# A convolution and feed-forward kernel on one core: the first windows of x, the dummies and the copies of the prologue in another order

## The chip, the cores and the metric

The kernel runs on one core of a Trainium2 chip. Its metric is the device time of one execution in microseconds (us). A core has five engines with a queue each: TensorE (PE in the profile; PEld is its loading of stationary operands), VectorE (DVE), ScalarE (ACT), GpSimd (POOL) and SyncE (SP). They run side by side and wait for each other by semaphores. Besides, 16 DMA engines move data. The letter q behind an engine's name stands for its instruction sequencer.

## The reference

```python
def _attn_ref(x, weight):                  # x: (8, 3904, 192), weight: (8 heads, 7 taps)
    w = softmax(weight, over the taps)
    x_pad = zeros(6 rows) + x              # along the sequence
    out[b, s, h, g] = sum_k w[h, k] * x_pad[b, s + k, h, g]        # 24 channels per head

def _moe_ref(x, w1, w2, w3, w_out):        # x: (31232, 192), d_ff = 1024
    a = x @ w1
    b = x @ w2
    h = a * b @ w3
    return h @ w_out
```

A causal depthwise convolution of 7 taps goes first, then a product of two projections, then two matrices that can be multiplied with each other ahead of time. All inputs and the output are float32; the kernel computes in bfloat16 and accumulates in float32.

## The kernel before

The 31232 tokens are cut into two streams of 15616 (`NS = 2`, index r). In most tiles the two streams sit side by side, one on each half of the partitions. The work runs in rounds R of 512 tokens per stream.

**Convolution.** x comes in windows of 32 rows that overlap by 6, so that each gives 26 new tokens. A banded 32x32 matrix per head, `Aband`, is the stationary operand (`conv`, L275); it is built in the prologue from the softmax of the taps: `share`, `spread` (PE, L215), `wsb`, `cprod`, `bps` (PE, L236), and the copy to `Aband` by VectorE at L240. The result in PSUM (`cps`) is copied to `convo` (L283). Windows go in batches; batch 0 has 20 windows per stream, all in one tile `xb`.

**The first windows of batch 0.** Windows below `HW = 8` come as float32 over SP's queue into the tile `begin`: window 0 apart (L149, 26 rows, since 6 rows are zeros set by VectorE at L141) and windows 1 to 7 in one transfer (L144), each for both streams. Three casts at L232 take them into `xb`: ScalarE casts stream 0 whole and the second half of stream 1, VectorE the first half of stream 1. Windows 8 to 19 come over POOL's queue straight into `xb` (L117, cast on the way), and behind them the weights `wn` (L187 to L190). In VectorE's queue the cast of L232 stands right ahead of the copy to `Aband`.

**Transposes.** The convolution's result is turned for the first product. For batch 0, `first_transposes` (L332) has a PSUM tile `tps` for each of three groups of channels k; for batches 1 and 2, `pe_transposes` (L317) puts the 15 transposes of all three groups in one tile `tps`, and three copies (L330) take them to `xT[0]` (VectorE), `xT[1]` (ScalarE) and `xT[2]` (VectorE), in this order. Later batches go through DRAM and DMA transposes.

**First product** (`first_product`, L378): for each of 8 blocks of 128 hidden channels, `pa` and `pb` (6 matmuls each, two streams side by side on half of the rows), `pa` copied to `asb` by ScalarE (L385), `abT = asb * pb` by VectorE (L387). Since the streams sit on different halves of the partitions, each weight tile `wn[k]` has an exchanged twin `ws` (`swap_w`, L181: two copies of 64x256 per stretch of columns). **Second product** (`second_product`, L403): `abT` times the folded `W_sb`. The fold of w3 and w_out (`w3_transpose` L448/L451, `w3_product` L460) is spread over rounds 1 and 2.

**PSUM.** All PSUM tiles are taken in turn from four buffers (`banks`); a PE group waits until the copy that reads the tile four places earlier is done.

**Order.** It is written out by hand (`tc.manual_schedule()`): each engine's queue holds its instructions in the order of the code. `first_product(R, between)` calls the entries of `between` behind the given block. `warm(n, wd)` (L192, matmuls at L195) issues n dummy matmuls on zeros.

Of the kernel before, what the change touches and what calls it, by code (L numbers as in the profile page):

```python
# [16 lines left out]
def kernel(  # L17
# [10 lines left out]
    nc = tc.nc  # L28
# [8 lines left out]
    NS = 2  # L37
# [6 lines left out]
    NP = D // Q  # L44
    C = 32
    ST = C - PAD
# [6 lines left out]
    NB = len(SIZES)  # L53
    FIRST = [sum(SIZES[:b]) for b in range(NB)]
    MAXN = 20
    HW = 8

    def tok(i):
        return (i // WB) * S + (i % WB) * ST
# [8 lines left out]
    def banks(name):  # L68
        return psum.tile([128, NS, CH], FP32, tag="banks", name=name)

    def banks_bf16(name):
        return psum.tile([128, 16, 128], BF16, tag="banks", name=name)
# [8 lines left out]
    def shape_of(b):  # L81
        n = SIZES[b] // 4
        m = n // (1 if b < 3 else 2)
        return n, m, n // m
# [6 lines left out]
    def group(r, e):  # L91
        return slice((2 * r + e) * C, (2 * r + e) * C + C)

    def runs_of(b, js, e):
        n, m, E = shape_of(b)
        runs = []
        for s, i in enumerate(FIRST[b] + j * n + u * E + e for j in js for u in range(m)):
            if i < HW or i == NWIN - 1:
                continue
# [37 lines left out]
    nc.scalar.dma_start(out=taps, in_=weight)  # L137
    begin = work.tile([128, HW, D], FP32, tag="abT", bufs=LAG + 1, name="begin")
    zeros = const.tile([128, CH], BF16)
    nc.vector.memset(zeros, 0.0)  # L140
    nc.vector.memset(begin[:, 0, :], 0.0)  # L141
    for r in range(NS):
        p = group(r, 0).start
        nc.sync.dma_start(out=begin[p:p + C, 1:HW, :], in_=bass.AP(  # L144
            tensor=x.tensor, offset=(r * TS + ST - PAD) * D,
            ap=[[D, C], [ST * D, HW - 1], [1, D]]))
    for r in range(NS):
        p = group(r, 0).start
        nc.sync.dma_start(out=begin[p + PAD:p + C, 0, :], in_=x_rows[r * TS:r * TS + ST, :])  # L149

    diag = const.tile([128, 128 + 8], BF16)
# [2 lines left out]
        out=diag, in_=diag, pattern=[[-1, 128 + 8]], compare_op=ALU.is_equal,  # L154
# [13 lines left out]
    for i in range(4):  # L168
        d = diag[i * C:i * C + C, i * C + 2 * i:i * C + 2 * i + C]
        nc.vector.tensor_copy(  # L170
            out=cmask[i * C:i * C + C],
            in_=bass.AP(tensor=d.tensor, offset=d.offset, ap=[d.ap[0], [1, 2], [1, C]]))
# [6 lines left out]
    def swap_w(k, lo, hi, f, halves=(1, 0)):  # L179
        for h in halves:  # L180
            f(out=wsw[k][Q * h:Q * h + Q, lo:hi], in_=wn[k][Q - Q * h:2 * Q - Q * h, lo:hi])  # L181

    V, A, P = nc.vector.tensor_copy, nc.scalar.copy, nc.gpsimd.tensor_copy
# [8 lines left out]
    def warm(n, wd=CH):  # L192
        t = banks("warm")
        for j in range(n):
            nc.tensor.matmul(t[:, j % 2, 0:wd], zeros[:, 0:128], zeros[:, 0:wd],  # L195
                             start=True, stop=True)

    warm(6)

    low = const.tile([H, 1], FP32)  # L200
    total = const.tile([H, 1], FP32)
# [3 lines left out]
    for i in range(4):  # L205
        ps = slice(i * C, i * C + C)
        nc.vector.tensor_copy(out=every[ps],
                              in_=diag[ps, ps].unsqueeze(1).to_broadcast([C, 4, C]))
    nc.vector.reciprocal(out=total, in_=total)
    nc.vector.scalar_tensor_tensor(  # L210
        out=share[:, :, 0:K], in0=taps.unsqueeze(1).to_broadcast([H, H, K]), scalar=total,
        in1=diag[0:H, 0:H].unsqueeze(2).to_broadcast([H, H, K]), op0=ALU.mult, op1=ALU.mult)
    spread = banks("spread")
    for i in range(4):
# [5 lines left out]
        out=wsb, in_=spread[:, 0, 0:2 * H].rearrange("p (h k) -> p h k", h=H)  # L220
# [5 lines left out]
        out=cprod.rearrange("p h k (s two) -> p h k s two", two=2),  # L226
# [3 lines left out]
        op=ALU.mult)  # L230
    for r, w0, w1, f in ((0, 0, HW, A), (1, HW // 2, HW, A), (1, 0, HW // 2, V)):
        f(out=xb_of[0][0][0][group(r, 0), w0:w1, :], in_=begin[group(r, 0), w0:w1, :])  # L232
    Aband = const.tile([128, H, C], BF16)
    bps = banks("bps")
    for k in range(2):
# [3 lines left out]
            start=(k == 0), stop=(k == 1))  # L239
    nc.vector.tensor_copy(out=Aband,  # L240
                          in_=bps[:, 0, 0:C * H].rearrange("p (h s) -> p h s", s=C))
    warm(3, 256)
    swap_w(0, 0, 256, V)


    xT = [const.tile([128, RING], BF16, name=f"xT{k}", tag=f"xT{k}") for k in range(NP)]
# [4 lines left out]
    def segments(c0, n):  # L251
        out = []
        while n:
            m = min(n, Q - c0 % Q)
            out.append((c0 // Q, c0 % Q, m))
            c0, n = c0 + m, n - m
        return out

    def conv(b, h0, nh, evict=(nc.scalar.copy,), es=None):
        n, m, E = shape_of(b)  # L260
        es = range(E) if es is None else es
        if b not in convo_of:
            convo_of[b] = work.tile([128, n, NP, NS, Q], BF16, tag="convo", bufs=2, name="convo")
            heads_left[b] = H * E
        convo = convo_of[b]
        wd = nh * G
        cps = {e: banks("cps") for e in es}
        for q in range(nh):
            cs = slice((h0 + q) * G, (h0 + q + 1) * G)
            for j in range(4):  # L270
                xb, s = xb_of[b][j]
                for e in es:
                    for r in range(NS):
                        o = cps[e][j * C:j * C + C, r, 0:m * wd]
                        nc.tensor.matmul(  # L275
                            o.rearrange("p (w g) -> p w g", g=wd)[:, :, q * G:(q + 1) * G],
                            Aband[group(r, e), h0 + q, :], xb[group(r, e), s:s + m, cs],
                            start=True, stop=True)
        for f, e in zip(evict, es):
            src = cps[e][:, :, 0:m * wd].rearrange("p r (w g) -> p r w g", g=wd)  # L280
            o = 0
            for k, c0, c in segments(h0 * G, wd):
                f(out=convo[:, e::E, k, :, c0:c0 + c]  # L283
                    .rearrange("p w r g -> p r w g"), in_=src[:, :, :, o:o + c])
                o += c
        heads_left[b] -= nh * len(es)
        if not heads_left[b]:
            del xb_of[b]
# [28 lines left out]
    def pe_transposes(b):  # L317
        n = SIZES[b] // 4
        convo = convo_of[b]
        tps = banks_bf16("tps")  # L320
        for k in range(NP):
            for w in range(n):
                nc.tensor.transpose(
                    out=tps[:, k * n + w, :],
                    in_=convo[:, w, k].rearrange("p r g -> p (r g)"), identity=ident)
        t0 = tok(FIRST[b])
        for k in range(NP):
            dst = xT[k][:, t0:t0 + 4 * n * ST].rearrange("p (c w s) -> p c w s", c=4, w=n)
            src = tps[:, k * n:(k + 1) * n, :].rearrange("p w (c s) -> p c w s", c=4)
            (nc.scalar.copy if k == 1 else nc.vector.tensor_copy)(out=dst, in_=src[:, :, :, 0:ST])  # L330

    def first_transposes():  # L332
        n = SIZES[0] // 4
        convo = convo_of[0]
        for k, f in enumerate((nc.scalar.copy, nc.vector.tensor_copy, nc.vector.tensor_copy)):
            tps = banks_bf16("tps")
            for w in range(n):
                nc.tensor.transpose(  # L338
                    out=tps[:, w, :],
                    in_=convo[:, w, k].rearrange("p r g -> p (r g)"), identity=ident)  # L340
            f(out=xT[k][:, 0:4 * n * ST].rearrange("p (c w s) -> p c w s", c=4, w=n),
              in_=tps[:, 0:n, :].rearrange("p w (c s) -> p c w s", c=4)[:, :, :, 0:ST])
# [125 lines left out]

    conv(0, 0, 4, evict=(A,))
    conv(0, 4, 4, evict=(V,))  # L470
    warm(2)
    first_transposes()
    for k, h in ((2, 1), (1, 1), (2, 0)):
        swap_w(k, 0, 256, A, (h,))
    swap_w(1, 0, 256, V, (0,))
    for k in (0, 2):
        swap_w(k, 256, HC, V)
    load_x(1)
# [20 lines left out]
    def later_loads():  # L499
# [10 lines left out]
        4: seq((conv, 1, 0, 4)),  # L510
        5: seq((conv, 1, 4, 4)),
        6: seq((pe_transposes, 1)),
        7: seq((conv, 2, 0, 4))})
    first_product(1, {
        0: seq((conv, 2, 4, 4)),
        2: seq((pe_transposes, 2), (store, 2, LAG_ROWS // ST)),
        3: seq((fold, 0)),
        6: seq((fold, 2)),
# [81 lines left out]
```

## Time and profile before

| what | us |
|---|---|
| median of 3 runs | 527.73 (527.26 to 529.17) |
| the profiled execution | 528.4 |
| its span, first to last instruction | 526.7 |
| PE busy | 519.4 |
| VectorE busy | 343.5 |
| ScalarE busy | 335.7 |

The profiled execution is 1.7 us longer than its span, and 0.67 us over the median. In the timeline of the profile each row has a start and a duration in us from the span's beginning, the engine, the line, the operation with its shapes, the count, and in brackets how long the engine sat idle before it and what ended that.

### The profile page before, as it was taken

How to read it: one execution, taken by the hardware profiler on the slowest of the kernel's cores; microseconds unless marked ns; L12 is line 12 of the kernel's file. 1: busy time of each engine (PE TensorE's matmuls, PEld its weight loads, DVE VectorE, ACT ScalarE, POOL GpSimd, SP SyncE). 2: the span in 40 equal slices, each digit the busy share in tenths (PEclk: the TensorE clock that was granted, in tenths of full speed). 3: DMA queues.
4: the chain of work that ended last, by engine and by line, in shares of the span. 5: the costliest groups of instructions: out<-in, count | busy, mean ns of one | idle time of the engine just before them, and what ended most of it. 6: DMA issues, size and time to landing. Idle time of an engine off the chain costs nothing.

```text
span 526.7 us, 14829 instructions
## 1 busy us (share of the span) xinstructions
PE 519.4 (99%) x6464; PEld 339.3 (64%) x6464; DVE 343.5 (65%) x326; ACT 335.7 (64%) x385; POOL 67.9 (13%) x127
## 2 busy tenths in 40 slices
PE   8999999999999999999999999999999999999997
PEld 4455775856758466584765847658475584856777
DVE  6776549578394774938759296592956929468380
ACT  6867567576574766747667475675757647466462
POOL 8746002004020010301102010020000000000000
PEclk9999999999999999999999999999999999999999
DMA  9999969966699476994779847797417543140304
GB/s 138 168 199 188 149 144 158 146 154 76 152 149 167 94 94 136 131 184 91 106 145 157 138 94 105 143 141 146 68 47 145 114 127 92 61 106 2 121 1 151
DMA packets 135351, 64.88 MB, mean 123 GB/s; under 512 B 87680, under 2 KB 134262, under 8 KB 135286
## 3 DMA queue, kind: packets, MB, share of 16 engines
q1 hardware_dynamic: 92838, 46.02, 42.0%
q0 software_dynamic: 42432, 17.92, 30.8%
q8 instruction: 50, 0.82, 0.6%
q14 instruction: 15, 0.12, 0.1%
q10 hardware_dynamic: 16, 0.00, 0.0%
HBM read 36.22 MB, written 34.80 MB: 135 GB/s over the span
## 4 chain that ended last, share of the span: by engine, by line
PE 93%; DVE 3%; ACT 2%; issue 1%; DMA 1%; SPq 0%; DVEq 0%
PE ops L403 31%; PE pa L378 29%; PE pb L378 28%; PE cps L275 3%; DVE abT L387 2%; ACT asb L385 1%; PE wps L460 1%; DMA begin<-in_x_dram 1%; PE w3ps L448 1%; PE tps L338 0%; ACT convo L283 0%; DVE ws L181 0%; PE ops L421 0%; DVE w3T L451 0%; PE warm L195 0%
## 5 line engine op out<-in xcount | busy, mean ns | idle before, releaser
L387 DVE TENSOR_TENSOR abT<-asb,pb 128x1024 bf16<-128x1024 bf16 x240 | 292.9, 1221 | 85.4 <-ACT asb L385 69.2
L385 ACT CAST asb<-pa 128x1024 bf16<-128x1024 f32 x244 | 247.1, 1013 | 65.6 <-PE pa L378 65.5
L378 PE MATMUL pb<-xT,wn 64*128 64x512 bf16 (+1 forms) x744 | 198.3, 373 | 0.6 <-DVE w3T L451 0.3
L378 PE MATMUL pa<-xT,wn 64*128 64x512 bf16 (+1 forms) x744 | 197.5, 373 | 0.9 <-DVE xT L330 0.6
L378 PE MATMUL pa<-xT,ws 64*128 64x512 bf16 (+1 forms) x744 | 197.6, 373 | 0.0
L378 PE MATMUL pb<-xT,ws 64*128 64x512 bf16 (+1 forms) x744 | 195.9, 373 | 0.0
L378 PEld LDWEIGHTS <-wn 64*128 64x128 bf16 x1488 | 138.0, 94 | 85.0 <-issue 2.4
L378 PEld LDWEIGHTS <-ws 64*128 64x128 bf16 x1488 | 131.2, 94 | 72.5 <-issue 2.1
L403 PE MATMUL ops<-W_sb,abT 128*128 128x192 bf16 x1936 | 166.8, 246 | 0.0
L403 PEld LDWEIGHTS <-abT 128*128 128x128 bf16 x1936 | 157.7, 98 | 9.3 <-issue 9.0
L408 ACT COPY osb<-ops 128x768 f32<-128x768 f32 (+1 forms) x61 | 48.4, 794 | 109.7 <-PE ops L403 109.7
L283 DVE CAST convo<-cps 128x320 bf16<-128x320 f32 (+4 forms) x44 | 31.5, 749 | 75.2 <-PE cps L275 75.2
L117 POOL DMA_DIRECT2D xb<-in_x_dram x74 | 48.3, 659 | 13.7 <-DMA xb<-in_x_dram 5.4
L283 ACT CAST convo<-cps 128x640 bf16<-128x640 f32 (+4 forms) x60 | 34.6, 623 | 0.9 <-PE cps L275 0.7
L555 POOL COPY pace<-abT 1x2 bf16<-1x2 bf16 x9 | 1.6, 176 | 252.4 <-DVE abT L387 252.4
L275 PE MATMUL cps<-xb,Aband 32*32 32x240 bf16 (+2 forms) x1344 | 17.1, 242 | 0.8 <-DVE Aband L240 0.6
L275 PEld LDWEIGHTS <-Aband 32*32 32x32 bf16 x1344 | 10.0, 89 | 9.0 <-issue 7.7
L425 DVE COPY osb<-ops 128x192 f32<-128x192 f32 x1 | 0.4, 358 | 11.7 <-PE ops L421 11.7
L195 PE MATMUL warm<-zeros 128*128 128x512 bf16 (+1 forms) x13 | 5.7, 579 | 1.3 <-DVE zeros L140 1.3
L460 PEld LDWEIGHTS <-w3T 128*128 128x128 bf16 x64 | 5.2, 98 | 1.8 <-issue 1.7
L451 DVE COPY w3T<-w3ps 128x2048 bf16<-128x2048 bf16 x4 | 4.9, 1223 | 1.9 <-PE w3ps L448 1.9
L460 PE MATMUL wps<-wo_b,w3T 128*128 128x192 bf16 x64 | 6.0, 246 | 0.2 <-DVE abT L387 0.2
(59 smaller groups left out, 64.5 us busy)
## 6 DMA issues: line engine op xcount, KB each, us to landing
out_dram<-osb SPq DMA_DIRECT2D x60, 384.0 KB
xb<-in_x_dram POOLq DMA_DIRECT2D x44, 240.0 KB, 7.6
rows<-convo SPq DMA_DIRECT2D x18, 240.0 KB
rows<-convo SPq DMA_DIRECT2D x18, 150.0 KB
w3b<-in_moe_w_dram POOLq DMA_DIRECT2D x8, 256.0 KB, 9.2
xT<-rows SPq DMA_TRANSPOSE x84
rows<-convo SPq DMA_DIRECT2D x11, 120.0 KB
xb<-in_x_dram POOLq DMA_DIRECT2D x4, 228.0 KB, 4.5
```

The source lines that it names most:

```text
L117: nc.gpsimd.dma_start(out=xb[group(r, e), s:s + w, :], in_=bass.AP(tensor=x.tensor, offset=(r * TS + t - PAD) * D, ap=[[D, C], [E * ST * D ...
L195: nc.tensor.matmul(t[:, j % 2, 0:wd], zeros[:, 0:128], zeros[:, 0:wd], start=True, stop=True)
L275: nc.tensor.matmul(o.rearrange("p (w g) -> p w g", g=wd)[:, :, q * G:(q + 1) * G], Aband[group(r, e), h0 + q, :], xb[group(r, e), s:s + m, ...
L283: f(out=convo[:, e::E, k, :, c0:c0 + c] .rearrange("p w r g -> p r w g"), in_=src[:, :, :, o:o + c])
L378: nc.tensor.matmul(p[:, r, f * N:f * N + N], w_of(i, k, r)[rs, ft * 128:(ft + 1) * 128], xT[k][rs, r0:r0 + N], start=(k == 0), stop=(k == ...
L385: nc.scalar.copy(out=asb[:, :, 0:per * N], in_=pa[:, :, 0:per * N])
L387: nc.vector.tensor_tensor(out=ab[:, f0, :, 0:N], in0=asb[:, :, 0:N], in1=pb[:, :, 0:N], op=ALU.mult)
L403: nc.tensor.matmul(ops[:, g // 2, (g % 2) * D:(g % 2) * D + D], ab[:, jt, r, g * 128:(g + 1) * 128], W_sb[:, jt, :], start=(jt == 0), stop ...
L408: nc.scalar.copy(out=osb.rearrange("p (a g) d -> p a (g d)", g=2), in_=ops[:, 0:ng // 2, 0:2 * D])
L448: nc.tensor.transpose(out=tps[:, q * JT + gt, :], in_=w3b[:, gt * 128:(gt + 1) * 128], identity=ident)
L451: nc.vector.tensor_copy(out=w3T_of[j0].rearrange("p q g c -> p (q g) c"), in_=tps)
L460: nc.tensor.matmul(wps[:, q, 0:D], w3T[:, q, gt, :], wo_b[:, gt, :], start=(gt == 0), stop=(gt == JT - 1))
```

## The change

- `HW` is 6: windows 6 and 7 of both streams come over POOL's queue (14 windows instead of 12 in each of its two transfers), windows 0 to 5 over SP's.
- SP's queue takes stream 0's two transfers first, then stream 1's two; before, it took the two large ones first and then the two small ones.
- One dummy of 256 columns is added behind the first six, and one more to the three behind `bps`.
- The exchange of weight 0's first 256 columns stood in VectorE's queue ahead of its copies of `convo`; now one half stands behind ScalarE's copies of `convo` and one behind VectorE's.
- Of the four exchanges behind `first_transposes`, ScalarE did three and VectorE one; now it is two and two.
- In `pe_transposes` the copies go in the order k = 1 (ScalarE), 2, 0 (VectorE).

```diff
-    HW = 8
+    HW = 6
...
     for r in range(NS):
         p = group(r, 0).start
         nc.sync.dma_start(out=begin[p:p + C, 1:HW, :], in_=...)
-    for r in range(NS):
-        p = group(r, 0).start
         nc.sync.dma_start(out=begin[p + PAD:p + C, 0, :], in_=x_rows[r * TS:r * TS + ST, :])
...
     warm(6)
+    warm(1, 256)
...
     nc.vector.tensor_copy(out=Aband, ...)
-    warm(3, 256)
-    swap_w(0, 0, 256, V)
+    warm(4, 256)
...
-        for k in range(NP):
+        for k, f in ((1, A), (2, V), (0, V)):
             ...
-            (nc.scalar.copy if k == 1 else nc.vector.tensor_copy)(out=dst, in_=src[:, :, :, 0:ST])
+            f(out=dst, in_=src[:, :, :, 0:ST])
...
     conv(0, 0, 4, evict=(A,))
     conv(0, 4, 4, evict=(V,))
+    swap_w(0, 0, 256, A, (0,))
+    swap_w(0, 0, 256, V, (1,))
     warm(2)
     first_transposes()
-    for k, h in ((2, 1), (1, 1), (2, 0)):
-        swap_w(k, 0, 256, A, (h,))
-    swap_w(1, 0, 256, V, (0,))
+    for k in (2, 1):
+        swap_w(k, 0, 256, A, (1,))
+    for k in (1, 2):
+        swap_w(k, 0, 256, V, (0,))
```

## The prediction

> **What bounds the kernel now.** I read the page first, then the waits of PE, then the timeline of the first 36 us engine by engine, then the DMA issues.
>
> ```profile
> PE 519.4 (99%) x6464; PEld 339.3 (64%) x6464; DVE 343.5 (65%) x326; ACT 335.7 (64%) x385; POOL 67.9 (13%) x127
> PE 93%; DVE 3%; ACT 2%; issue 1%; DMA 1%; SPq 0%; DVEq 0%
> ```
>
> PE is busy 519.4 of 526.7 us, and the windows of 10 us show 10.00 in each from 60 to 100 us (the page has nines to the end). The change adds PE nothing there, so all that it can move lies in PE's holes before 36 us. The waits of PE list them:
>
> ```profile
> PE pa L378 <- DVE xT L330: 0.6, 1, 0.6
> PE cps L275 <- DVE Aband L240: 0.6, 1, 0.6
> PE pb L378 <- DVE w3T L451: 0.3, 1, 0.3
> PE pb L378 <- DVE abT L387: 0.3, 1, 0.3
> PE cps L275 <- DVE abT L387: 0.2, 1, 0.2
> ```
>
> The timeline shows what stands before them. First the prologue:
>
> ```profile
> 4.62 2.32 ACT L232 CAST xb<-begin 32x1536 bf16<-32x1536 f32 x2 [1.40 <-DMA begin<-in_x_dram]
> 5.82 0.55 DVE L232 CAST xb<-begin 32x768 bf16<-32x768 f32 x1 [0.84 <-DMA begin<-in_x_dram]
> 6.40 0.42 DVE L240 CAST Aband<-bps 128x256 bf16<-128x256 f32 x1
> 6.88 1.11 PE L275 MATMUL cps<-xb,Aband 32*32 32x120 bf16 x64 [0.57 <-DVE Aband L240]
> 7.93 1.03 PE L195 MATMUL warm<-zeros 128*128 128x512 bf16 x2
> 8.75 1.81 PE L338 MATMUL tps<-diag,convo 128*128 128x128 bf16 x15
> 10.94 2.08 DVE L181 COPY ws<-wn 64x256 bf16<-64x256 bf16 x5
> 13.05 3.52 DVE L387 TENSOR_TENSOR abT<-asb,pb 128x1024 bf16<-128x1024 bf16 x3
> ```
>
> The convolution starts at 6.88, behind three things that end together: Aband (6.82), ScalarE's casts (6.94), and POOL's second transfer of x0. The DMA issues give that last one:
>
> ```profile
> xb<-in_x_dram POOLq DMA_DIRECT2D x2, 144.0 KB, 4.6
> ```
>
> The two issues start at 1.51 and 2.32 us and land 4.6 us later, at 6.1 and 6.9. Behind the transposes, VectorE makes five exchanges up to 13.02, and its first abT (13.05 to 14.28) releases the buffer of the third pb: PE waits 0.27 us to 14.33. Then the end of round 0:
>
> ```profile
> 22.04 1.22 DVE L387 TENSOR_TENSOR abT<-asb,pb 128x1024 bf16<-128x1024 bf16 x1 [0.66 <-ACT asb L385]
> 23.18 0.42 DVE L330 COPY xT<-tps 128x520 bf16<-128x520 bf16 x1
> 23.63 0.59 ACT L330 COPY xT<-tps 128x520 bf16<-128x520 bf16 x1 [1.63 <-DVE xT L330]
> 24.26 0.43 DVE L330 COPY xT<-tps 128x520 bf16<-128x520 bf16 x1 [0.66 <-ACT xT L330]
> 24.12 1.02 ACT L385 CAST asb<-pa 128x1024 bf16<-128x1024 f32 x1
> 24.74 0.37 PE L378 MATMUL pa<-xT,wn 64*128 64x512 bf16 x1 [0.58 <-DVE xT L330]
> ```
>
> The three copies from one tps run one after the other across the two engines. ScalarE is free from 22.01 but waits 1.63 us, since VectorE's copy of k = 0 must go first and itself waits for an abT. PE then waits for tps to come free.
>
> **The copies of pe_transposes.** With k = 1 first, ScalarE copies as soon as the transposes end (22.43): 22.55 to 23.15. VectorE ends its abT at 23.26 and makes k = 2 and 0 back to back by 24.05 (2 x 0.42). Its turn on ScalarE costs no one, and k = 0 coming last delays no matmul: tps is free at 24.05 instead of 24.69, before PE's 24.16. That removes PE's 0.58. ScalarE's asb follows at 23.2, as soon as pa is done, instead of 24.12; the next abT ends near 25.5, not 26.39, which removes the 0.23 ahead of cps. So 0.8 us here. What is late next is the abT behind the next asb: about 0.1 to 0.2 comes back. In round 1 the same chain stands from 31.33 to 32.85 (ScalarE waits 1.63 again), delays asb from 31.5 to 32.28, abT to 34.55, w3T to 35.69, and PE: pa starts at 34.60 instead of 34.34, pb at 35.74 instead of 35.25. Those 0.26 + 0.49 go too, less about 0.05 for w3T. Sum: 0.81 + 0.75 - 0.15, **-1.4 us**. Bounds: 0 (the wait comes back elsewhere) and -1.6.
>
> **x0.** SP's queue loses 128 rows, POOL's two transfers gain 64 each. POOL's issue time does not grow (0.7 us for the 20 windows of a later load, 0.6 to 0.8 here). SP: stream 0's small transfer now waits for VectorE's zeroing (ends 1.43) with stream 1's two queued behind it, 0.2 us late; only the casts of stream 1 wait for these. Stream 0 lands no later than its 4.55 (nothing of stream 1 lies ahead). ScalarE's casts of 1536 and 768 elements take 1.47 and 0.83 us, so 1152 and 576 take 1.15 and 0.67: done by 6.44, off the path. VectorE's cast shrinks from 0.55 to about 0.45; it starts with stream 1's small transfer, 5.72 before, now between 5.2 and 5.9, so Aband comes between 6.1 and 6.8. That frees two of the three. The third is POOL's second transfer: its 384 rows landed 0.83 us behind the first's, so 128 more rows cost 128/384 x 0.83 = 0.28 us, to 7.2. Bounds: -0.35 (Aband alone decides), and 0.95 by the pace of the first 384 rows (their packets begin at 3.26 in the trace's packet records and land at 6.10: 128/384 x 2.84). I take the pace of the second, which is the nearest row: with the turn-on of the first matmuls, **+0.3 us**. All that follows is PE at its pace: convolution, two dummies, transposes.
>
> The Trainium skill ("DMA: Bandwidth & Descriptors", Issuing engines are not separate DMA queues) says that DMAs of SP and GpSimd run on the same 16 engines and interleave. By that alone the 1268 rows are as many as before, the transfer lands at 6.9 again and the term is 0 instead of +0.3. The trace's packet records agree on the sharing, but SP's large transfers are over when POOL's begin, so rows moved behind 3.26 us lengthen the busy part.
>
> **The exchanges.** Weight 0's: VectorE began convo at 8.09, right behind the convolution's end (7.99), so its move gains at most 0.1, under PE's transposes (8.75 to 10.56), and costs nothing: ScalarE is free from 8.67 to 9.53 for a 0.40 copy, VectorE from 9.30 to 10.06. Without that cover it would be 0.4. Behind the transposes VectorE gets a sixth copy of the kind that takes 0.42 with about 0.04 between: its first abT starts 0.4 later, and with it the third pb, where PE already waits. **+0.4 us** (0 if VectorE's copies speed up to the 0.22 of its shortest one; 0.46 at most). ScalarE's lost copy frees time that nobody waits for.
>
> **Dummies.** The first (0.21 us) fills PE's idle time before spread, 3.83 to 4.08; the second reaches 6.31, and the convolution isn't ready before 6.5. Zero; uncovered 0.2 each.
>
> **Sum.** -1.4 + 0.3 + 0.4 = -0.7 us on the profiled 528.4. That execution lies 0.67 over the median of the runs; I take the difference off the median: 527.73 - 0.7 = 527.0 us.
>
> **Rivals.**
>
> *The clock comes up earlier.* PE begins at half pace: 15 transposes take 1.81 us at 8.75, and as many 1.00 at 21.43 (L323). Full pace comes near 10.7, that is 3.8 us of unbroken work behind the hole that ends at 6.88. With the new dummies PE works from 1.27 to 6.31 without a hole, 5.0 us. If that suffices, the convolution's 64 matmuls take 0.72 (as at 63.12), the dummies 0.43, and VectorE's evictions become the limit: xT[2] about 0.7 earlier than before instead of 0.3 later, 1.0 us better than my sum: 526.0. Against: before the hole at 3.83 (0.25 us) and after it there were 4.8 us of nearly full work too.
>
> *The clock comes up later, and the result is slower.* If the 3.8 us count from PE's last hole, and the later x0 opens a new one between the transposes and the first pa (xT[0] lands just then, 10.4 against 10.7), full pace comes near 14.5 instead of 10.7: 3.6 us at half pace cost 1.8. Then 528.8. It decides from a rise at about 12.2 on.
>
> The Trainium skill ("TensorE: Matmul & The Clock Gate", The HAM clock gate) lets the clock rise at the end of a busy window of about 3.4 us that runs free of the kernel's start. By it the rise would come a whole window earlier or later than 10.7 by chance of phase, as the two rivals have it. The single rise in this trace fits but cannot show the phase.
>
> *x0 is not later.* Then the term is 0 to -0.35: 526.4 to 526.7. For: VectorE and ScalarE no longer hold the start. Against: the queue count above.
>
> *The new order of the copies does not help*, as abT or ScalarE's asb hold PE all the same: -1.4 falls away, 528.4. Against: the 1.63 us on ScalarE's row name VectorE alone.
>
> **Chances.** My sum 0.42, earlier clock 0.2, x0 not later 0.13, later clock 0.12, copies without gain 0.13. Range: from the earlier clock with x0 at -0.3 (526.0 - 0.6 = 525.4, 0.3 less for the spread of runs) to the later clock, 528.8, 0.3 more: 525.1 to 529.1. A measurement of this kernel can tell about 0.5% (2.6 us) from no change. Faster by that needs under 525.1, earlier clock and every bound at its best: 0.08. Slower needs over 530.4, the later clock and no gain from the copies: 0.06. Within: 0.86.
>
> **What would show it.** Right: ScalarE's xT copies with no 1.63 us wait, PE's waits on xT and w3T gone, POOL's x0 landing near 7.2, VectorE six exchanges and PE's wait at the third pb grown to about 0.7. Wrong: the 15 first transposes in about 1.0 us (earlier clock), the first pa blocks at 1.3 us each (later clock), or x0 landing at 6.9 or before.

## The result and the profile after

| | before | changed |
|---|---|---|
| median, us | 528.37 (527.26 to 530.04, 6 runs) | 525.93 (525.43 to 526.14, 6 runs) |
| profiled execution, us | 528.4 | 525.43 |
| its span, us | 526.7 | 523.7 |
| PE busy, us | 519.4 | 518.1 |

The changed kernel takes 0.995 of the time before (95% interval 0.9932 to 0.9968), 2.4 us less. The forecast of 527.0 had the direction and held the time in its range (525.1 to 529.1), but it was 1.1 us too high, and two of its four terms were wrong. Measured as a saving it was further off: 0.7 us were forecast and 2.4 measured. The forecast went out from the median of three runs, 527.73, and with six runs the kernel before is at 528.37; that the base was 0.64 lower than this hides part of the error, which is luck.

PE's waits after the change, in the profiled execution, which is the fastest of the six:

```profile
PE warm L193 <- DVE zeros L140: 1.3, 1, 1.3
PE pb L376 <- DVE abT L385: 0.2, 1, 0.2
PE wps L458 <- DVE abT L385: 0.2, 1, 0.2
PE warm L193 <- issue: 0.2, 1, 0.2
PE cps L273 <- issue: 0.2, 1, 0.2
```

The waits on Aband, on xT and on w3T are gone. (Lines have moved: L273 is the convolution, L336 the first transposes, L328 the copies of `pe_transposes`, L376 the first product, L383 asb, L385 abT, L179 the exchanges.) The prologue, from the timeline:

```profile
5.63 0.45 DVE L231 CAST xb<-begin 32x576 bf16<-32x576 f32 x1 [0.57 <-DMA begin<-in_x_dram]
6.11 0.42 DVE L239 CAST Aband<-bps 128x256 bf16<-128x256 f32 x1
6.59 0.74 PE L273 MATMUL cps<-xb,Aband 32*32 32x120 bf16 x64
...
7.40 1.22 DVE L281 CAST convo<-cps 128x320 bf16<-128x320 f32 x2 [0.86 <-PE cps L273]
...
7.85 1.28 PE L336 MATMUL tps<-diag,convo 128*128 128x128 bf16 x15
...
9.70 1.90 DVE L179 COPY ws<-wn 64x256 bf16<-64x256 bf16 x6
11.63 1.22 DVE L385 TENSOR_TENSOR abT<-asb,pb 128x1024 bf16<-128x1024 bf16 x1
...
12.91 0.37 PE L376 MATMUL pb<-xT,wn 64*128 64x512 bf16 x1 [0.20 <-DVE abT L385]
```

The convolution begins at 6.59 instead of 6.88, its 64 matmuls take 0.74 instead of 1.11, the first transposes 1.28 instead of 1.81, and the third pb starts at 12.91 instead of 14.33: the prologue alone is 1.4 us shorter in these two executions. They are not equal ones: the profile of before (528.4) is of an execution above the medians of before in the sets below (527.6 to 528.1), that of the changed kernel of its fastest. In the changed one the convolution starts behind Aband (6.53), as POOL's x0 has landed by 6.32. The DMA issues show POOL's x0:

```profile
xb<-in_x_dram POOLq DMA_DIRECT2D x2, 168.0 KB, 3.9
```

It carries 168 KB per transfer instead of 144, and yet lands 3.9 us after its issue instead of 4.6. Last, the end of round 0:

```profile
20.62 1.22 DVE L385 TENSOR_TENSOR abT<-asb,pb 128x1024 bf16<-128x1024 bf16 x1 [0.66 <-ACT asb L383]
21.76 0.76 DVE L328 COPY xT<-tps 128x520 bf16<-128x520 bf16 x2
...
21.05 0.59 ACT L328 COPY xT<-tps 128x520 bf16<-128x520 bf16 x1 [0.46 <-PE tps L321]
21.80 1.01 ACT L383 CAST asb<-pa 128x1024 bf16<-128x1024 f32 x1 [0.17 <-PE pa L376]
```

ScalarE waits for PE's transposes alone, no longer 1.63 us for VectorE. VectorE makes its two copies in a row, and asb follows pa at once.

The profiles of all 14 kernels (the two above and the twelve below) can be cut at the start of the third pb. From there to the end of the execution (the profiled time less that start) lie 528.40 - 14.33 = 514.1 us before and 525.43 - 12.91 = 512.5 us changed. In the four kernels with the old order of the copies it is 514.1 to 514.4, in the ten with the new order 512.5 to 513.1. So what the copies save, some 1.5 us, lies behind the third pb. What the other parts do shows mainly in the start of the third pb, which lies anywhere from 12.83 (after_again) to 15.12 (copies_alone).

### The profile page after: what moved, and what is told of

It is laid out like the page before. It is cut to its first block, busy times and chain, and to the rows that moved or that the text cites. A ratio compares the mean times of both kernels' runs of the same rounds, so it can differ in the third digit from the quotient of the medians.

```text
span 523.7 us, 14832 instructions
## 1 busy us (share of the span) xinstructions
PE 518.1 (99%) x6465; PEld 337.7 (64%) x6466; DVE 343.2 (66%) x326; ACT 335.3 (64%) x385; POOL 67.7 (13%) x127
## 4 chain that ended last, share of the span: by engine, by line
PE 96%; DVE 2%; ACT 1%; issue 0%; DVEq 0%
PE ops L401 31%; PE pa L376 30%; PE pb L376 29%; PE cps L273 3%; PE wps L458 1%; DVE abT L385 1%; PE warm L193 1%; PE w3ps L446 1%; ACT asb L383 1%; PE tps L321 0%; DVE ws L179 0%; PE ops L419 0%; DVE convo L281 0%; ACT convo L281 0%; DVE xT L339 0%
## 5 line engine op out<-in xcount | busy, mean ns | idle before, releaser
L385 DVE TENSOR_TENSOR abT<-asb,pb 128x1024 bf16<-128x1024 bf16 x240 | 293.0, 1221 | 85.2 <-ACT asb L383 68.5
L383 ACT CAST asb<-pa 128x1024 bf16<-128x1024 f32 x244 | 247.1, 1013 | 66.0 <-PE pa L376 65.8
L376 PE MATMUL pb<-xT,wn 64*128 64x512 bf16 (+1 forms) x744 | 198.2, 373 | 0.2 <-DVE abT L385 0.2
L376 PE MATMUL pa<-xT,wn 64*128 64x512 bf16 (+1 forms) x744 | 197.6, 373 | 0.2
L376 PE MATMUL pa<-xT,ws 64*128 64x512 bf16 (+1 forms) x744 | 197.7, 373 | 0.0
L376 PE MATMUL pb<-xT,ws 64*128 64x512 bf16 (+1 forms) x744 | 196.0, 373 | 0.0
L376 PEld LDWEIGHTS <-wn 64*128 64x128 bf16 x1488 | 137.8, 94 | 85.1 <-issue 2.3
L376 PEld LDWEIGHTS <-ws 64*128 64x128 bf16 x1488 | 131.2, 94 | 71.2 <-ACT asb L383 0.5
L273 PE MATMUL cps<-xb,Aband 32*32 32x240 bf16 (+2 forms) x1344 | 16.9, 238 | 0.2 <-issue 0.2
L273 PEld LDWEIGHTS <-Aband 32*32 32x32 bf16 x1344 | 9.8, 88 | 8.5 <-issue 7.0
```

The source lines that it names most:

```text
L273: nc.tensor.matmul(o.rearrange("p (w g) -> p w g", g=wd)[:, :, q * G:(q + 1) * G], Aband[group(r, e), h0 + q, :], xb[group(r, e), s:s + m, ...
L376: nc.tensor.matmul(p[:, r, f * N:f * N + N], w_of(i, k, r)[rs, ft * 128:(ft + 1) * 128], xT[k][rs, r0:r0 + N], start=(k == 0), stop=(k == ...
L383: nc.scalar.copy(out=asb[:, :, 0:per * N], in_=pa[:, :, 0:per * N])
L385: nc.vector.tensor_tensor(out=ab[:, f0, :, 0:N], in0=asb[:, :, 0:N], in1=pb[:, :, 0:N], op=ALU.mult)
```

## The experiments

Twelve kernels ran, in three sets of four. Each set is measured beside its own runs of the kernel before on the same chip (medians 527.72, 528.12 and 527.60 us), so the ratios to these runs are the surest numbers. The yardstick for the changed kernel is the run `after_again` of the second set (525.76). The first and the third set hold no run of the changed kernel, so their differences to it go across chips, and are uncertain by some 0.5 us, which is how far the medians of before lie apart.

### The parts alone, and the dummies taken out

**copies_alone**: the kernel before with the order of the copies only.

```diff
-        for k in range(NP):
+        for k, f in ((1, A), (2, V), (0, V)):
```

> The kernel before with the new order of the three copies in pe_transposes alone. Theory (the copies are worth 1.4 us, as in the forecast's sum): 1.2 to 1.6 us faster than before, ScalarE's 1.63 us waits ahead of xT gone, PE's waits on xT (0.58) and w3T (0.31) gone, the first 20 us of the profile as before. Rival (the waits come back as waits for abT or asb): less than 0.5 us faster, with new waits of PE between 24 and 36 us.

Measured 526.37 us, ratio 0.9972 (0.9962 to 0.9983), which is 1.5 us on 527.72. The term of -1.4 us holds (by the interval 0.9 to 2.0). Its profile happens to show the slowest of its 12 executions (527.69), and that shows a second thing. From the timeline:

```profile
5.34 2.32 ACT L232 CAST xb<-begin 32x1536 bf16<-32x1536 f32 x2 [2.12 <-DMA begin<-in_x_dram]
...
7.72 0.99 PE L275 MATMUL cps<-xb,Aband 32*32 32x120 bf16 x63 [0.64 <-ACT xb L232]
...
9.47 1.81 PE L338 MATMUL tps<-diag,convo 128*128 128x128 bf16 x15
```

and from its windows (from:to, length, then busy time of PE, PEld, DVE, ACT and POOL; the column behind POOL's is the granted clock):

```profile
3.00:4.00 1.00, 1.00 (x3) 0.16 (x2) 0.92 (x4) 0.23 (x2) 1.00 (x2) 1.00 1.14 145
4.40:7.40 3.00, 1.39 (x8) 0.66 (x7) 1.53 (x4) 2.03 (x2) 2.59 (x6) 1.00 1.28 172
8.00:10.50 2.50, 2.17 (x69) 1.72 (x51) 1.28 (x3) 1.27 (x3) 2.50 (x4) 0.50 1.10 165
11.50:13.00 1.50, 1.50 (x16) 0.68 (x14) 1.41 (x5) 1.25 (x3) 1.31 (x4) 1.00 1.34 147
```

Stream 0's small transfer landed late (the cast waits 2.12 us, not 1.40), PE stood idle for more than half of 4.4 to 7.4, and the clock fell to half for what followed. (The column has no entry before the first recorded step of the clock: the first window's 1.00 is none.) The trace's clock records give steps at 4.36 (up), 7.78 (down) and 11.19 us (up): 3.41 us apart each time.

**dummies_alone**: the kernel before with the two dummies only.

```diff
     warm(6)
+    warm(1, 256)
...
-    warm(3, 256)
+    warm(4, 256)
```

> The kernel before with the two added dummies alone (one of 256 columns ahead of spread, one behind bps). Theory (unbroken work of PE up to about 6.3 us raises the clock, whatever stands behind): the 15 first transposes take 1.3 us or less instead of 1.81, and the kernel is 0.5 to 1.0 us faster than before. Rival (the hole ahead of the convolution must go too, and the dummies leave some 0.35 us of it): transposes at 1.8 us, within 0.2 us of before.

527.47 us, ratio 0.9995 (0.9984 to 1.0006): no difference that can be told. In its profile the clock did rise early (record at 6.42) and the transposes took 1.41 us, but the executions are spread as before (527.21 to 529.66). Neither reading is fully right: the early rise is there in this one execution, the gain in the median is not.

**x0_alone**: HW = 6 and SP's order only, on the kernel before.

```diff
-    HW = 8
+    HW = 6
...
-    for r in range(NS):
-        p = group(r, 0).start
         nc.sync.dma_start(out=begin[p + PAD:p + C, 0, :], ...)
```

> The kernel before with HW = 6 and SP's new order alone. Theory (SP's rows are out of the way, POOL's second transfer of x0 lands near 6.3 as in the changed kernel): the convolution starts at 6.6 or before and the kernel is 0.3 to 0.5 us faster; if the shorter hole ahead of the convolution also raises the clock, 1.0 to 1.5 us. Rival (the forecast's step: 128 more rows in POOL's queue land later): POOL's second transfer at 7.1 to 7.2, convolution complete 0.3 us later, kernel 0.3 us slower.

527.60 us, ratio 0.9997 (0.9985 to 1.0008), though x0 landed at 6.28 and the convolution began at 6.52. VectorE's timeline shows one place where it is held up:

```profile
7.38 0.46 DVE L179 COPY ws<-wn 64x256 bf16<-64x256 bf16 x2 [0.91 <-DMA wn<-in_moe_w_dram]
7.75 1.21 DVE L281 CAST convo<-cps 128x320 bf16<-128x320 f32 x2
```

Weight 0 lands at 7.35. Its exchange, still ahead of the copies of convo here, holds them until 7.75, where the changed kernel starts them at 7.40. PE then waits 0.20 for convo ahead of the third group of transposes. So this exchange, left where it was, takes 0.35 us of the earlier x0 back at this point. At the third pb 0.2 of it is left in the profiles (13.10 here, 12.91 in the changed kernel). No run moves that exchange alone, so what its move is worth in the median is not shown. Nor does the earlier x0 alone narrow the spread: two of the 12 executions are at 528.51 and 529.82.

**no_dummies**: the changed kernel without the two added dummies.

> The changed kernel without the two added dummies. Theory (the dummies raise the clock): the 15 first transposes take 1.8 us again, full pace comes near 10.7, and the kernel is 0.7 to 1.0 us slower than the changed one, that is about 1.4 to 1.7 us faster than before. Rival (the earlier x0 closes the hole and raises the clock without them): transposes at 1.3 us, time as the changed kernel, 2.4 us faster than before.

526.08 us (525.75 to 526.75), ratio 0.9965 (0.9954 to 0.9977), about 0.3 us over `after_again` and within the uncertainty. The transposes take 1.28 us as in the changed kernel and the clock rose at 6.29: about the clock the rival was right. The time does not decide: it is 1.8 us under before (1.2 to 2.4), where the theory had 1.4 to 1.7 and the rival 2.4. So the two dummies can be worth a few tenths, not the 0.7 to 1.0 of the theory.

### The changed kernel with one part taken back

**after_again**: the changed kernel once more.

> The changed kernel once more, on the chip of the three runs beside it, as their yardstick and for a second look at its clock. Theory (the clock's windows of 3.4 us run free of the kernel): full pace comes at another time than 6.6, anywhere between 4.3 and 8, and the time is again 0.4 to 0.6% under before. Rival (the dummies fix the moment): full pace at 6.5 to 6.7 again.

525.76 us (525.35 to 526.31), ratio 0.9955 (0.9943 to 0.9967). The clock record has the rise at 6.19, not at 6.59: the moment moves from execution to execution, as the theory had it.

**old_copies**: the changed kernel with the old order of the copies.

```diff
-        for k, f in ((1, A), (2, V), (0, V)):
+        for k in range(NP):
```

> The changed kernel with the old order of the three copies in pe_transposes. Theory (the copies are 1.4 to 1.5 us of the whole, as they were alone): 1.4 us slower than the changed kernel, 0.9 to 1.1 us faster than before, and PE's waits on xT and w3T are back. Rival (the parts overlap): under 1.0 us slower than the changed kernel.

527.52 us, ratio 0.9986 (0.9977 to 0.9995): 1.8 us slower than `after_again`, and the waits of before are back, from PE's waits:

```profile
PE pa L376 <- DVE xT L328: 0.6, 1, 0.6
PE pb L376 <- DVE w3T L449: 0.3, 1, 0.3
PE cps L273 <- DVE abT L385: 0.2, 1, 0.2
```

**x0_as_before**: the changed kernel with HW = 8 and SP's old order (the edit of x0_alone reversed).

> The changed kernel with HW = 8 and SP's old order. Theory (with the other parts in place the earlier x0 pays, which it could not do alone behind VectorE's exchanges): convolution complete 0.3 to 0.7 us later, kernel 0.4 to 0.7 us slower than the changed one, and its slowest executions above 527 us, since a longer hole ahead of the convolution lets the clock fall or stay low. Rival (x0 is worth nothing here either): within 0.2 us of the changed kernel.

526.47 us, ratio 0.9975 (0.9963 to 0.9988): 0.7 us slower than `after_again`, or 1.1 by the ratios, and 5 of its 12 executions lie above 527 us (up to 528.55), where the changed kernel stays under 526.4 in all of its 11. That is the theory's outcome, but not by its path in the profiled execution (526.28), a faster one: there POOL's x0 landed at 6.45, and the convolution began at 6.58, no later than in the changed kernel. Its 64 matmuls took 0.91 us instead of 0.74, and the third pb began at 13.19, some 0.3 us late.

**three_on_scalar**: ScalarE makes three of the four exchanges again.

```diff
-    for k in (2, 1):
-        swap_w(k, 0, 256, A, (1,))
-    for k in (1, 2):
-        swap_w(k, 0, 256, V, (0,))
+    for k, h in ((2, 1), (1, 1), (2, 0)):
+        swap_w(k, 0, 256, A, (h,))
+    swap_w(1, 0, 256, V, (0,))
```

> The changed kernel with ScalarE making three of the four exchanges behind the first transposes again. The forecast's step says that the sixth exchange on VectorE costs 0.4 us: then this is 0.4 us faster than the changed kernel. Theory now (PE waits only 0.20 us at the third pb, and ScalarE has 0.48 us free ahead of its first asb): 0.2 us faster, the wait at the third pb gone, the first abT no later than 0.1 us behind the first asb. Rival (ScalarE's asb starts later in exchange): no difference or 0.2 us slower.

525.77 us, ratio 0.9953 (0.9941 to 0.9964): the same as `after_again` (525.76). No cost of the sixth exchange on VectorE can be told; with an interval of 0.6 us to either side neither 0.2 nor 0.4 us is ruled out by the times. PE still waits 0.3 at the third pb, so the theory's step, that this wait goes, did not come true.

### x0 taken apart, one attempt to go further, and no dummies

**old_sp_order**: the changed kernel with SP's old order, HW = 6 kept.

```diff
+    for r in range(NS):
+        p = group(r, 0).start
         nc.sync.dma_start(out=begin[p + PAD:p + C, 0, :], ...)
```

> The changed kernel with SP's old order (both large transfers first), HW = 6 kept. Theory (14 windows per transfer spread evenly over the DMA engines, 12 do not: that is why POOL's x0 lands early): POOL's second transfer lands at 6.2 to 6.4 as in the changed kernel, its 16 completions within 0.7 us of each other; time within 0.3 us of the changed kernel. Rival (SP's order is what clears the way): it lands at 6.6 or later, completions spread over 1 us or more, 0.4 us slower.

526.23 us (526.04 to 526.40), ratio 0.9972 (0.9961 to 0.9983). POOL's second transfer landed at 6.72, its 16 completions within 0.69 us. The even spread is as the theory has it, the landing and the time are the rival's. Yet the landing is not the whole reason for the time. The convolution began at 6.52 in this execution, no later than in the changed kernel, and what came late is the third pb:

```profile
10.02 2.40 DVE L181 COPY ws<-wn 64x256 bf16<-64x256 bf16 x6
...
13.73 0.37 PE L378 MATMUL pb<-xT,wn 64*128 64x512 bf16 x1 [0.71 <-DVE abT L387]
```

VectorE began its six exchanges 0.32 us later than in the changed kernel (9.70), 0.57 us ahead of POOL's own (10.59) instead of 0.97, and took 2.40 us for them instead of 1.90.

**eight_new_order**: the changed kernel with HW = 8, SP's new order kept.

> The changed kernel with HW = 8, SP's new order kept. Theory (the even spread of 14 windows): POOL's second transfer lands at 6.4 to 6.9, its completions spread over 1 us or more, and the kernel is 0.3 to 0.7 us slower than the changed one. Rival (SP's order): lands at 6.2 to 6.4, time as the changed kernel.

526.21 us (525.84 to 527.34), ratio 0.9976 (0.9967 to 0.9985); landed at 6.83, completions over 0.93 us. That is near the theory, but SP's order alone does not help either. So taking back either half of x0 costs some 0.3 to 0.5 us by the medians and 0.9 to 1.1 by the ratios, not clearly less than taking back both. The halves differ in the tail: with 8 windows 3 of 10 executions lie above 526.9, with 6 none of 6. Its profile, of the slowest execution (527.34), has the clock's three steps again: up at 4.00, down at 7.42, up at 10.83. What kept the convolution back there was not POOL's x0 but Aband: VectorE's cast of x0 ahead of it could begin only at 6.08, and PE sat idle for 1.25 us:

```profile
7.14 0.88 PE L273 MATMUL cps<-xb,Aband 32*32 32x120 bf16 x64 [1.25 <-DVE Aband L239]
```

**scalar_casts**: the last cast of x0 on ScalarE, and three dummies behind bps.

```diff
-    for r, w0, w1, f in (..., (1, 0, HW // 2, V)):
+    for r, w0, w1, f in (..., (1, 0, HW // 2, A)):
...
-    warm(4, 256)
+    warm(3, 256)
```

> The changed kernel with the last cast of x0 (first half of stream 1) on ScalarE too, so that VectorE makes Aband without waiting for x0, and three dummies instead of four behind bps. Theory (the cast ahead of Aband and the fourth dummy hold the convolution, at 6.5 to 6.6): it starts at 6.3 to 6.45, held by POOL's x0, and the kernel is 0.1 to 0.3 us faster than the changed one. Rival (VectorE's later work sets the pace): same time.

525.94 us, ratio 0.9962 (0.9948 to 0.9975): not faster than the changed kernel. The convolution begins at 6.41 as foreseen, but VectorE's later work sets the pace, from the timeline:

```profile
9.68 2.40 DVE L179 COPY ws<-wn 64x256 bf16<-64x256 bf16 x6
12.11 3.48 DVE L385 TENSOR_TENSOR abT<-asb,pb 128x1024 bf16<-128x1024 bf16 x3
...
13.39 0.37 PE L376 MATMUL pb<-xT,wn 64*128 64x512 bf16 x1 [0.71 <-DVE abT L385]
```

The same six exchanges take 2.40 us instead of 1.90: POOL's own exchanges began at 10.25 here, at 10.67 in the changed kernel.

**no_dummies_at_all**: the changed kernel without any `warm`.

> The changed kernel without any dummy matmul. Theory (a slow clock in the first product is what dummies save): full pace comes between 10 and 14 us, the 15 first transposes take 1.8 us, and the kernel is 1.5 to 2.5 us slower than the changed one. Rival (VectorE and ScalarE are the limit up to 13 us anyway): under 1.0 us slower.

527.37 us (526.20 to 527.83), ratio 0.9987 (0.9977 to 0.9996), 1.4 to 1.6 us over the changed kernel. The clock record has the rise at 13.73 and the transposes take 1.78, as the theory said. That is what all dummies together save.

## Why the prediction was right or wrong, point by point

**Copies of pe_transposes: right.** -1.4 was forecast; alone they gave 1.5 us by the ratio, within the changed kernel 1.8 by the medians. Each step is in the profile: ScalarE's 1.63 us gone, the copies of VectorE in a row, asb at 21.80 behind pa, and no new wait in PE's list. The rival that abT or asb would hold PE all the same fell: behind the third pb all four kernels with the old order take at least 0.9 us longer than all ten with the new one.

**x0: wrong.** The failing step is "I take the pace of the second": 128 rows more at the pace of the last 384 were to bring the landing from 6.9 to 7.2. It came at 6.3, and the convolution started at 6.59 instead of 6.88, near my bound of -0.35, where Aband alone decides. The rate I took was not that of the queue but of its stragglers. The trace's completion records show it (16 for each transfer): with 12 windows per transfer the first and last completion of POOL's second one lie 0.93 to 1.50 us apart (five executions of five kernels), with 14 windows 0.21 to 0.69 us (eight executions of eight kernels that have dummies). In the packet records 768 rows of 12 windows thin out from 5.25 us on, to 23 per 0.25 us at 6.25, while the 896 rows of 14 windows run at 98 to 124 per 0.25 us from 4.00 to 5.75, and 16 are left. Why 12 windows spread less evenly over the engines is not shown. The rule of the Trainium skill ("DMA: Bandwidth & Descriptors", Issuing engines are not separate DMA queues) gave 6.9 as the prediction worked it out, by the equal number of rows, and was nearer than I, but did not have the gain either. SP's order seems to add its part: with 14 windows and the old order the landing was 6.72. That rests on one execution, and in another, x0_as_before, 12 windows with the old order landed at 6.45; so the even spread is shown in all 13, the earlier landing only with SP's new order.

**Dummies: right as far as the runs can tell.** Zero was forecast; alone they gave 0.3 us (-0.3 to 0.8), and the changed kernel without them is some 0.3 us slower, within the uncertainty.

**Exchanges: wrong by size in the changed kernel.** The term of +0.4 took every copy on VectorE at 0.42. That duration belongs to VectorE beside POOL's copies. In the changed kernel, by the line's own view from 0 to 10.6 and from 10.6 to 20 us (minimum/median/maximum in ns):

```profile
L179 DVE COPY ws<-wn x5: 221/224/316, 8.7 to 10.4; 64x256 bf16<-64x256 bf16 x5
...
L179 DVE COPY ws<-wn x3: 316/424/447, 10.4 to 11.2; 64x256 bf16<-64x256 bf16 x3
```

(One that crosses 10.6 stands in both.) POOL's copies start at 10.67. Before, VectorE's exchanges began at 10.94 and met them nearly all; now most are done first, six in 1.90 us instead of five in 2.08. My lower bound of 0 named just this 0.22 and I did not ask when POOL starts. `scalar_casts` and `old_sp_order` show the reverse: where POOL's copies meet more of the six, they take 2.40 us, and PE's wait at the third pb is 0.71, just what the prediction named. So the price is real, and the changed kernel escapes most of it only by where POOL happens to be.

**The exchange of weight 0: no cost seen, worth missed.** The profile of the changed kernel shows no wait for it, but "gains at most 0.1" was reckoned for a convolution that ends at 7.99. With the earlier x0 it holds VectorE to 7.75 (x0_alone), 0.35 us later than the changed kernel. That it is worth as much is argued from this one profile.

**The clock: the earlier rise came, and the weights of the rivals were off.** In the profiled execution of the changed kernel the rise came at 6.59, as in the rival of 526.0. The rule of the Trainium skill ("TensorE: Matmul & The Clock Gate", The HAM clock gate), windows of some 3.4 us that run free of the kernel, agrees with the runs: steps 3.41 us apart in two kernels, and the rise of the same kernel at 6.59 and 6.19. Against it stood my "3.8 us of unbroken work", which was only the phase of one execution: `dummies_alone`, `x0_alone` and `no_dummies` rose at 6.42, 6.03 and 6.29. Nor is the rise bound to 10.7 plus or minus a whole window, as the prediction read it: in the twelve other kernels with dummies the first rise came anywhere from 4.00 to 7.06. It was the profile of before, with 10.72, that was the exception. A later rise, the other rival, shows in neither of the changed kernel's two profiles. The dummies do not decide this alone. What the change removes, as far as the profiles go, are the bad phases: where PE has a long hole ahead of the convolution, the clock fell back to half (copies_alone, eight_new_order) or stayed low (the profile of before with its rise at 10.7). The kernel before has executions from 527.1 to 530.0, the changed one from 525.35 to 526.31. That the whole upper end of that spread has this cause is argued from the three that were profiled, not shown for each. Against it stand x0_alone (up to 529.82) and dummies_alone (up to 529.66), which shorten the hole and keep the spread; none of their longest executions was profiled. Which parts must come together to narrow it is open.

**Sum.** Between the lowest executions (527.11 and 525.35) lie 1.8 us, of which the copies are 1.5; between the medians 2.4, since the tail is gone as well. The forecast took x0 and the exchanges for losses of 0.7 together. They were none, and what is left beside the copies, about 0.9, is the gain of x0, the exchanges, the dummies and the clock together; how it divides among them is not shown. The time, 525.93, is that of the rival of the earlier clock (526.0, chance 0.2), but its reason, PE's unbroken work through the new dummies, is not what the runs show: without them (no_dummies) the clock rose at 6.29.

## What to carry to other kernels

Where several engines read one PSUM tile in turn, put first the reader whose engine is free, and let the busy engine take the rest in a row: that was 1.5 of 2.4 us here. A start-up is worth judging by its spread as well as its median: the parts together narrowed a spread that one profile shows only by chance. Before a copy is costed, look at what the neighbouring engine does at that moment: the same row of the profile held 0.22 and 0.42 us.

## What the runs showed of the hardware that was not expected

- A PE clock that had risen at 4.36 us fell back to half at 7.78, though PE had never been idle for a whole window: 1.49 us of work in 3.41 (copies_alone). So it did with 1.94 of 3.41 us (eight_new_order, 4.00 to 7.42). With 2.57 of 3.41 us it stayed (old_copies, 4.07 to 7.48).
- VectorE's copy of 64x256 bf16 takes 0.22 us at its shortest and 0.42 to 0.46 beside POOL's copies of the same size (0.40 each); ScalarE's takes 0.40 in both cases. A few of VectorE's took 0.28 to 0.41 ahead of POOL's copies, while POOL was issuing loads (0.41 at 10.16 in old_sp_order, where POOL's copies begin at 10.59).
- The completions of a DMA transfer of 448 rows lay closer together than those of one of 384 rows from the same queue (0.21 to 0.69 against 0.93 to 1.50 us). With SP's new order the larger pair also landed earlier, at 6.2 to 6.5 against 6.8 us.
